# Attention by head pairs on fp16 high and low halves, and experts in tiles of 640 rows

## The chip, the cores and the metric

One core of a Trainium2 chip runs the whole program. The metric is the device time in microseconds. Five engines work from queues of their own: TensorE (PE in the profile, its weight loads PEld), VectorE (DVE), ScalarE (ACT), GpSimd (POOL) and SyncE (SP, which here only starts transfers). Transfers run on 16 DMA engines that all queues share. Matrix products read SBUF and write PSUM, eight banks of 2 KB in each of 128 partitions; VectorE or ScalarE must bring the results out of it.

## The reference

Inputs q, k, v are fp32 of shape (8 batches, 8 heads, 576, 64). For each batch and head two attentions are added:

```
q_d, k_d, v_d = means over groups of 4 rows      # 144 rows
out_up    = repeat(softmax(q_d k_d^T / 8) v_d, 4)
out_local = softmax(q k^T / 8 where |i - j| < 4) v
x = (out_up + out_local) as (4608 tokens, 512)
e_idx  = argmax(x @ w_gate)                       # 8 experts
gate_w = softmax(x @ w_gate)[e_idx]; eom = sigmoid(x @ w_output_gate)
out[token] = gate_w * eom[e_idx] * (relu(x @ w1[e]) @ w2[e])   # w1 512x1024, w2 1024x512
```

Each token goes to the one expert that its largest logit names, so the gate's logits must be exact enough to keep the order of near ties. With the fixed inputs the reference sends 553, 637, 487, 619, 575, 566, 572 and 599 tokens to the experts.

## The kernel before

The program is written for a planner that tracks the buffers: it gives every engine its own order of instructions, starting from program order but bringing an instruction forward when its inputs and a free buffer are there in the planner's own account of time. On the chip each engine then takes its list in order. A pool's `bufs` says how many copies of a tile may be alive.

**Attention** (lines 213 to 314) runs over 8 batches and in each over 8 heads. `load_batch` (lines 184 to 211) brings one batch of q, k and v over the SP queue, one batch ahead; GpSimd casts q and k to fp16 (L198 to L201); v stays fp32 in six overlapping blocks of 128 rows. For each head TensorE transposes q and k (L226, L228), makes the local scores in six blocks of 102 by 96 (L239) and the scores of the means (L252, L254). ScalarE takes exponentials (L244, L257, L258), VectorE multiplies by a mask (L246). The products with v are fp32 (L249, L275 to L279); the means of v are fp32 products against a pooling matrix (L261), transposed again (L266, L267). The 144 coarse rows are split into fp16 high and low halves and spread to 576 rows by 14 matmuls with a 0/1 matrix (L296 to L303). VectorE normalizes and adds (L306 to L310). After 8 heads the batch goes to DRAM (L311).

**Gate** (`gate_tile`, lines 119 to 182): 36 tiles of 128 tokens read x back, transpose it in fp32, multiply by both gates in fp32 (L129), find the expert, count ranks with a triangular matrix (L163, L164), and scatter the scaled fp16 row to the expert's slots in `hx_xs` (L179), 1024 slots for each expert. A running count `r_run` ties every tile to the one before.

**Experts** (lines 319 to 361): all 1024 slots of each expert, in four blocks of 256 rows. Weights arrive as fp32 in a single staging tile (`wst`, bufs=1) and are cast by ScalarE (L325) and VectorE (L329). `pye` has one buffer, copied by VectorE (L359). Results go to `hx_ys`.

**Gather** (lines 362 to 367): 36 times, an indirect read of 128 rows of `hx_ys` and a plain write to `out`, through four buffers.

Of the kernel before, what the change touches and what calls it, by code (L numbers as in the profile page):

```python
# [8 lines left out]
F32 = mybir.dt.float32  # L10
F16 = mybir.dt.float16
BF16 = mybir.dt.bfloat16
I32 = mybir.dt.int32
U32 = mybir.dt.uint32
# [4 lines left out]

def _ap(t, ap_list, extra_off=0):  # L20
    return bass.AP(tensor=t.tensor, offset=t.offset + extra_off, ap=ap_list)


@with_exitstack
def kernel(
# [16 lines left out]
    CAP = 1024  # L42
    NB = 6
    BR = 96
    KJ = BR + 6
    SD = S // 4
    scale = 1.0 / (D ** 0.5)
    NSLOT = CAP * E
    NT = N // 128

    x_dram = nc.dram_tensor("hx_x", (N, Dm), F32, kind="Internal")
    xs_dram = nc.dram_tensor("hx_xs", (NSLOT, Dm), F16, kind="Internal")
    ys_dram = nc.dram_tensor("hx_ys", (NSLOT, Dm), F32, kind="Internal")

    x5 = x_dram.ap().rearrange("(b t r) (h d) -> b r t h d", b=B, t=NB, r=BR, h=H)
# [10 lines left out]
    maskL = cst.tile([128, NB, BR], F32)
    nc.gpsimd.memset(maskL, 1.0)
    nc.gpsimd.affine_select(out=maskL, in_=maskL, compare_op=ALU.is_ge, fill=0.0,
                            base=0, pattern=[[0, NB], [-1, BR]], channel_multiplier=1)
    nc.gpsimd.affine_select(out=maskL, in_=maskL, compare_op=ALU.is_ge, fill=0.0,  # L70
                            base=6, pattern=[[0, NB], [1, BR]], channel_multiplier=-1)
    nc.gpsimd.affine_select(out=maskL, in_=maskL, compare_op=ALU.is_ge, fill=0.0,
                            base=-3, pattern=[[96, NB], [0, BR]], channel_multiplier=1)
    nc.gpsimd.affine_select(out=maskL, in_=maskL, compare_op=ALU.is_ge, fill=0.0,
                            base=S + 2, pattern=[[-96, NB], [0, BR]], channel_multiplier=-1)

    rall = cst.tile([128, NB, BR], F16)
    nc.gpsimd.memset(rall, 0.0)
    nc.gpsimd.affine_select(out=rall.rearrange("p t (a r) -> p t a r", r=4),
                            in_=rall.rearrange("p t (a r) -> p t a r", r=4),  # L80
                            compare_op=ALU.not_equal, fill=1.0, base=0,
                            pattern=[[-24, NB], [-1, 24], [0, 4]], channel_multiplier=1)
    rall2 = cst.tile([128, BR], F16)
    nc.gpsimd.memset(rall2, 0.0)
    nc.gpsimd.affine_select(out=rall2.rearrange("p (a r) -> p a r", r=4),
                            in_=rall2.rearrange("p (a r) -> p a r", r=4),
                            compare_op=ALU.not_equal, fill=1.0, base=8,
                            pattern=[[-1, 24], [0, 4]], channel_multiplier=1)
    rb = cst.tile([128, 24], F32)
    nc.gpsimd.memset(rb, 0.25)  # L90
    nc.gpsimd.affine_select(out=rb, in_=rb, compare_op=ALU.is_ge, fill=0.0,
                            base=-3, pattern=[[-4, 24]], channel_multiplier=1)
    nc.gpsimd.affine_select(out=rb, in_=rb, compare_op=ALU.is_ge, fill=0.0,
                            base=6, pattern=[[4, 24]], channel_multiplier=-1)
    lstr = cst.tile([128, 128], BF16)
    make_upper_triangular(nc, lstr, val=1.0, diag=False)
    ones128 = cst.tile([128, 128], BF16)
    nc.gpsimd.memset(ones128, 1.0)
    iota8i = cst.tile([128, 8], I32)
    nc.gpsimd.iota(iota8i, pattern=[[1, 8]], base=0, channel_multiplier=0)  # L100
    iota8f = cst.tile([128, 8], F32)
    nc.vector.tensor_copy(iota8f, iota8i)
    wgc = cst.tile([128, 4, 2 * E], F32)
    nc.sync.dma_start(wgc[:, :, 0:E], moe_w_gate.rearrange("(c p) e -> p c e", p=128))
    nc.sync.dma_start(wgc[:, :, E:2 * E], moe_w_output_gate.rearrange("(c p) e -> p c e", p=128))
    pos_all = cst.tile([128, NT], I32)
    zf16 = cst.tile([128, Dm], F16)
    nc.vector.memset(zf16, 0.0)
    nc.sync.dma_start(xs_dram.ap()[0:NSLOT, :].rearrange("(a p) d -> p a d", p=128),
                      _ap(zf16, [zf16.ap[0], [0, NSLOT // 128], [1, Dm]]))  # L110
    r_run = cst.tile([128, E], F32)
    nc.vector.memset(r_run, 0.0)
# [6 lines left out]
    def gate_tile(m):  # L119
        x128 = sbA.tile([128, Dm], F32, tag="x128")  # L120
        nc.sync.dma_start(x128, x_rt[m])
        pxT = psA.tile([128, 4, 128], F32, tag="pgate")
        for c in range(4):
            nc.tensor.transpose(pxT[:, c, :], x128[:, 128 * c:128 * c + 128], id32)
        xTs = sbA.tile([128, 4, 128], F32, tag="xTs")
        nc.vector.tensor_copy(xTs, pxT)  # L126
        pg = psA.tile([128, 2 * E], F32, tag="pgate")
        for c in range(4):
            nc.tensor.matmul(pg, lhsT=xTs[:, c, :], rhs=wgc[:, c, :],  # L129
                             start=(c == 0), stop=(c == 3))  # L130
        nlm = sbA.tile([128, 1], F32, tag="nlm")
        nc.vector.reduce_max(nlm, pg[:, 0:E], axis=AX.X, negate=True)
        pe8 = sbA.tile([128, E], F32, tag="pe8")
        sume = sbA.tile([128, 1], F32, tag="sume")
        nc.scalar.activation(pe8, pg[:, 0:E], AF.Exp, bias=nlm, scale=1.0, accum_out=sume)
        eomx = sbA.tile([128, E], F32, tag="eomx")
        nc.scalar.activation(eomx, pg[:, E:2 * E], AF.Exp, scale=-1.0)
        gw = sbA.tile([128, 1], F32, tag="gw")
        nc.vector.tensor_scalar_add(sume, sume, 1e-9)
        nc.vector.reciprocal(gw, sume)  # L140
        nc.vector.tensor_scalar_add(eomx, eomx, 1.0)
        eom8 = sbA.tile([128, E], F32, tag="eom8")
        nc.vector.reciprocal(eom8, eomx)
        mx8 = sbA.tile([128, 8], F32, tag="mx8")
        mi8 = sbA.tile([128, 8], U32, tag="mi8")
        nc.vector.max_with_indices(mx8, mi8, pg[:, 0:E])
        ef = sbA.tile([128, 1], F32, tag="ef")
        nc.vector.tensor_copy(ef, mi8[:, 0:1])
        onehot = sbA.tile([128, E], F32, tag="onehot")
        nc.vector.tensor_scalar(onehot, iota8f, scalar1=ef, scalar2=None, op0=ALU.is_equal)  # L150
        onehotb = sbA.tile([128, E], BF16, tag="onehotb")
        nc.vector.tensor_copy(onehotb, onehot)
# [64 lines left out]
    for b in range(B):  # L217
        q16, k16, vblk = pend
        if b + 1 < B:
            pend = load_batch(b + 1)  # L220
# [91 lines left out]
        for m in range(NT):  # L312
            if (128 * m + 127) // S == b:
                gate_tile(m)
# [83 lines left out]
```

## Time and profile before

| what | value |
|---|---|
| time, median of 3 runs | 1258.67 us (1256.92 to 1260.21) |
| profiled execution, span from first to last instruction | 1255.6 us |
| PE, PEld busy | 991.5 us (79%), 768.4 us (61%) |
| DVE, ACT, POOL busy | 523.1 us (42%), 246.2 us (20%), 117.6 us (9%) |
| instructions on PE | 6520 |
| moved by DMA | 141.63 MB, mean 113 GB/s |

The profiled execution has no time of its own besides its span, which is 3.1 us below the median of the timed runs; what lies around the span is thus about 3 us. Busy time is the union of an engine's instructions. Since matmuls overlap in the pipeline, a group's mean duration is longer than the distance between two starts; distances are read from the timeline.

### The profile page before, as it was taken

The page shows a single profiled execution, that of the slowest core. Times are in us where ns is not written, and L with a number is a line of the kernel's source. Part 1 is how long each engine was busy: PE and PEld are TensorE (multiplying, and loading weights), DVE is VectorE, ACT ScalarE, POOL GpSimd, SP SyncE. Part 2 cuts the span into 40 slices and gives each one's busy share as a digit, 9 for nine tenths or more (in the row PEclk, how much of TensorE's full clock was granted, in tenths as well). Part 3 has the DMA queues.
Part 4 walks back from the last instruction along what each step waited for, and adds up shares of the span by engine and source line. Part 5 has one row for each costly group of instructions (what it writes and reads, how often), then busy time and mean ns, then how long its engine had stood idle before and what let it go on. Part 6 is the DMA issues. An engine that isn't in the chain of part 4 may idle for free. (4 is left out here: it accounts for less than half of the span.)

```text
span 1255.6 us, 16704 instructions
## 1 busy us (share of the span) xinstructions
PE 991.5 (79%) x6520; PEld 768.4 (61%) x6520; DVE 523.1 (42%) x2211; ACT 246.2 (20%) x437; POOL 117.6 (9%) x128
## 2 busy tenths in 40 slices
PE   0799998899999987998899999864599999999000
PEld 0577776777787776777678777743366666666000
DVE  0354445545545555555655554634132323332000
ACT  0212211211321212221121121100133333322000
POOL 2310011010010002001100000001000000000243
PEclk9999999999999999999999999999999999999655
DMA  9940534616424332051040101011246666631677
GB/s 315 187 90 1 137 84 85 149 34 164 96 90 91 77 115 93 10 131 65 10 103 14 30 22 51 19 44 56 72 150 209 205 217 212 218 131 68 204 238 227
DMA packets 180991, 141.63 MB, mean 113 GB/s; under 512 B 126768, under 2 KB 143152, under 8 KB 180912
## 3 DMA queue, kind: packets, MB, share of 16 engines
q1 hardware_dynamic: 176304, 126.40, 35.4%
q0 software_dynamic: 4608, 14.16, 4.0%
q8 instruction: 51, 0.84, 0.3%
q14 instruction: 28, 0.23, 0.1%
HBM read 91.78 MB, written 48.76 MB: 112 GB/s over the span
## 5 line engine op out<-in xcount | busy, mean ns | idle before, releaser
L249 PE MATMUL ploc<-vblk,atl 102*96 102x65 f32 x768 | 146.8, 371 | 3.8 <-DVE atl L246 2.7
L357 PE MATMUL pye<-w2sb,hs 128*128 128x512 f16 x512 | 126.3, 379 | 20.9 <-DVE yee L359 19.9
L249 PEld LDWEIGHTS ploc<-vblk,atl 102*96 102x96 f32 x768 | 130.5, 275 | 14.2 <-DVE atl L246 5.8
L359 DVE COPY yee<-pye 128x512 f32<-128x512 f32 x64 | 44.2, 690 | 181.4 <-PE pye L357 181.4
L349 PE MATMUL phT<-xgT,w1sb 128*128 128x256 f16 x1024 | 118.9, 275 | 0.8 <-DVE xgT L342 0.8
L349 PEld LDWEIGHTS <-w1sb 128*128 128x128 f16 x1024 | 101.1, 99 | 20.2 <-issue 1.0
L226 PE MATMUL pqkt<-id,q 128*64 128x128 f16 (+1 forms) x320 | 81.1, 303 | 32.5 <-POOL q L198 32.5
L261 PE MATMUL pvdt<-rb,vblk 128*64 128x24 f32 x768 | 98.7, 283 | 8.5 <-ACT edt L258 8.0
L353 ACT ACTIVATE hs<-phT 128x1024 f16<-128x1024 f32 x64 | 65.5, 1023 | 193.4 <-PE phT L349 193.4
L235 DVE TENSOR_REDUCE qkd<-qkT 64x288 f16<-64x1152 f16 x64 | 84.7, 1324 | 38.2 <-ACT qkT L233 33.3
L261 PEld LDWEIGHTS pvdt<-rb,vblk 128*64 128x64 f32 x768 | 88.5, 222 | 17.5 <-ACT edt L258 12.6
L179 POOL DMA_INDIRECT hx_xs<-x16r,posi x36 | 35.1, 976 | 600.5 <-DVE pos_all L178 364.3
L357 PEld LDWEIGHTS <-hs 128*128 128x128 f16 x512 | 47.4, 97 | 69.5 <-issue 24.8
L233 ACT COPY qkT<-pqkt 64x1152 f16<-64x1152 f16 x64 | 70.8, 1106 | 82.6 <-PE pqkt L228 58.0
L296 PE MATMUL pup<-odh,rall 128*96 128x64 f16 x384 | 74.3, 265 | 15.5 <-DVE odh L290 10.4
L228 PE MATMUL pqkt<-id,k 128*64 128x128 f16 (+1 forms) x320 | 80.0, 299 | 5.4 <-POOL k L200 5.4
L129 PE MATMUL pg<-wgc,xTs 128*128 128x16 f32 x288 | 67.9, 376 | 16.2 <-DVE xTs L126 13.9
L129 PEld LDWEIGHTS pg<-wgc,xTs 128*128 128x128 f32 x288 | 64.2, 328 | 26.1 <-DVE xTs L126 20.9
L226 PEld LDWEIGHTS <-q 128*64 128x64 f16 (+1 forms) x320 | 47.9, 153 | 51.9 <-POOL q L198 32.5
L257 ACT ACTIVATE edt<-psd 128x144 f32<-128x144 f32 x64 | 18.5, 290 | 301.9 <-PE psd L254 301.9
L244 ACT ACTIVATE etl<-pst 102x576 f32<-102x576 f32 x64 | 41.5, 649 | 155.8 <-PE pst L239 148.9
L298 PE MATMUL pup<-odl,rall 128*96 128x64 f16 x384 | 69.5, 270 | 0.0
(116 smaller groups left out, 1456.6 us busy)
## 6 DMA issues: line engine op xcount, KB each, us to landing
w1st<-in_moe_w_dram SPq DMA_DIRECT2D x8, 2048.0 KB
w2st<-in_moe_w_dram SPq DMA_DIRECT2D x8, 2048.0 KB
hx_ys<-yee SPq DMA_DIRECT2D x8, 2048.0 KB, 13.8
hx_x<-out_sb SPq DMA_DIRECT2D x8, 1152.0 KB, 6.4
x<-hx_x SPq DMA_DIRECT2D x36, 256.0 KB, 2.7
out_dram<-g SPq DMA_DIRECT2D x36, 256.0 KB, 3.5
hx_xs<-zf SPq DMA_DIRECT2D x1, 8192.0 KB
q_rows<-in_q_dram SPq DMA_DIRECT2D x32, 256.0 KB, 4.8
```

The lines of the kernel that those rows point to most:

```text
L129: nc.tensor.matmul(pg, lhsT=xTs[:, c, :], rhs=wgc[:, c, :], start=(c == 0), stop=(c == 3))
L226: nc.tensor.transpose(pqkt[0:64, 0, 128 * m:128 * m + cnt], q16[0:cnt, h, m, :], id16[0:cnt, 0:cnt])
L228: nc.tensor.transpose(pqkt[0:64, 1, 128 * m:128 * m + cnt], k16[0:cnt, h, m, :], id16[0:cnt, 0:cnt])
L233: nc.scalar.copy(qkT[:, :, 3:579], pqkt[0:64, :, 0:576])
L235: nc.vector.tensor_reduce(qkd, qkT[:, :, 3:579].rearrange("p s (a r) -> p s a r", r=4), axis=AX.X, op=ALU.add)
L249: nc.tensor.matmul(ploc[:, t, :], lhsT=atl[0:KJ, t, :], rhs=vblk[0:KJ, h, t, :], start=True, stop=True)
L261: nc.tensor.matmul(pvdt[:, 24 * t:24 * t + 24], lhsT=vblk[:, h, t, 0:D], rhs=rb, start=True, stop=True)
L296: nc.tensor.matmul(pup[:, t, :], lhsT=rall[:, t, :], rhs=odh[0:128, 0, :], start=True, stop=False)
L298: nc.tensor.matmul(pup[:, t, :], lhsT=rall[:, t, :], rhs=odl[0:128, 0, :], start=False, stop=(t < 5))
L349: nc.tensor.matmul(phT[:, f4, :], lhsT=w1sb[:, c, 128 * f:128 * f + 128], rhs=xgT[:, :, c, :], start=(c == 0), stop=(c == 3))
L353: nc.scalar.activation(hs[:, 4 * half:4 * half + 4, :], phT, AF.Relu)
L357: nc.tensor.matmul(pye[:, rh, :], lhsT=hs[:, f, 128 * rh:128 * rh + 128], rhs=w2sb[:, f, :], start=(f == 0), stop=(f == E - 1))
```

## The change

Nearly the whole kernel is rewritten. The core of it, with `...` for what is left out:

```diff
+W = 112
+NB = 5
+Q0 = [0, 120, 232, 344, 456]
+QN = [120, 112, 112, 112, 120]
+CAPJ = 5
...
-    nc.sync.dma_start(xs_dram.ap()[0:NSLOT, :].rearrange("(a p) d -> p a d", p=128), ...
+    for r in range(E):                                  # 640 rows of 1032 bytes each
+        nc.scalar.dma_start(xs_dram.ap()[r * REG:r * REG + 128 * CAPJ, :]..., zt ...)
+    def load_weights(e):                                # wpool bufs=3
+        nc.gpsimd.dma_start(w1sb, moe_w1[e]...)         # fp32 in DRAM, fp16 in SBUF
+        nc.gpsimd.dma_start(w2sb, moe_w2[e]...)
+    def attn_pair(b, hp, vh, vdh, vdl, xo, vl):
+        pool_ps = psA.tile([128, 2, SD], F32, tag="M")
+        for i, src in enumerate((q, k)):
+            f = sbA.tile([96, 6, 2, D], F32, tag=f"qk{i}", bufs=3)
+            for h in range(2):
+                nc.sync.dma_start(f[:, :, h, :], src[b, h0 + h]...)
+            nc.gpsimd.tensor_copy(s16, f...)            # 96x768 to fp16
+            tp = psA.tile([128, S], F16, tag="T", bufs=2)
+            for m in range(6):
+                nc.tensor.transpose(tp[:, 96 * m:96 * m + 96], s16[:, m, :], id16[0:96, 0:96])
+            for m in range(6):
+                nc.tensor.matmul(pool_ps[:, i, 24 * m:24 * m + 24], lhsT=s16[:, m, :], rhs=pb[0:96, 0:24], ...)
+            nc.vector.tensor_copy(sT, tp)
+        nc.scalar.copy(qkd, pool_ps)
+        for h in range(2):       # pa: 1 mask matmul of 456 columns, 4 of about 114
+        for h in range(2):       # pbt: 1 mask matmul of 408, then 120, 144 and 144
...
+            nc.scalar.activation(E32[:, 0:NA], sc[h][:, 0:NA], AF.Exp, scale=scale)   # NA = 456
+            nc.scalar.activation(eh[:, 0:NA], sc[h][:, 0:NA], AF.Exp, scale=scale)
+            nc.scalar.activation(E32[:, NA:], pbt[:, 0:NBt], AF.Exp, scale=scale)     # NBt = 408
+            nc.scalar.activation(eh[:, NA:], pbt[:, 0:NBt], AF.Exp, scale=scale)
+            if h == 0:
+                nc.gpsimd.tensor_tensor(el, E32, eh, op=ALU.subtract)                 # 128x864
+            else:
+                nc.vector.tensor_tensor(el, E32, eh, op=ALU.subtract)
+            po = psA.tile([128, NB + 2, 65], F32, tag="O", bufs=2)
+            # 5 blocks x 3 and 2 x 2 x 3 matmuls, 64 or 65 columns: eh*vh, eh*vl, el*vh
+            nc.vector.reciprocal(rs, po[:, :, 64])
+            nc.vector.tensor_tensor(xo[:, :, D * hh:D * hh + D], po[:, :, 0:D], _bc(rs, D), op=ALU.mult)
+    def gate(b, xo):
+        for t in range(NB):      # spread of the coarse rows, SBUF to SBUF, 6 transfers
+            nc.sync.dma_start(up[0:4 * n, t, :], _ap(src, [src.ap[0], [0, 4], [1, Dm]]))
+        nc.vector.tensor_tensor(x, x, up, op=ALU.add)                                 # 120x2560
+        nc.scalar.copy(xh[0:BR, :, 0:Dm], x)
+        nc.gpsimd.tensor_tensor(xl[0:BR], x, xh[0:BR, :, 0:Dm], op=ALU.subtract)
+        # for t in 5: 8 transposes, 1 copy by VectorE, 8 matmuls of 32 or 16 columns
+        # then once for all 5: about 20 small operations of VectorE, 3 of ScalarE,
+        # 6 rank matmuls
+        for t in range(NB):
+            nc.gpsimd.indirect_dma_start(out=xs_dram.ap(), ... pos[:, t:t + 1] ..., in_=xh[0:P, t, :]...)
+    for b in range(B):
+        # per pair: 2 loads of v; GpSimd writes vh, VectorE vl
+        # 12 matmuls of 512 columns against pv: the means of v for all 8 heads
+        for hp in range(NP):
+            attn_pair(b, hp, vh, vd1h, vdl, xo, vl)
+        gate(b, xo)
+        if b < 3:
+            load_weights(b)
+    def experts(xgi, nj, w1sb, w2sb, group):            # nj = 5: 640 rows
+        # 20 transposes, 3 copies; 8 x 2 x 4 matmuls of 320 columns, buffers U bufs=4,
+        # relu by ScalarE for one half and VectorE for the other; 5 x 8 matmuls of 512
+        nc.scalar.activation(y[:, j, :], py, AF.Copy, scale=coef[:, j, 0:1])          # Y bufs=2
+        nc.gpsimd.indirect_dma_start(out=out_rows, ..., in_=y[:, j, :], ..., bounds_check=N - 1, oob_is_err=False)
+    for e in range(E):
+        if e not in wts:
+            load_weights(e)
+        nc.sync.dma_start(xg, xs_dram.ap()[base:base + 128 * CAPJ, :]...)
+        experts(xg, CAPJ, *wts[e], True)
+    v_most = nc.values_load(most[0:1, 0:1], ...)
+    with tc.If(v_most > 0):      # for an expert with more than 640 tokens: loops over more tiles
...
-        for m in range(NT):      # gather and write of out, and all of gate_tile, are gone
```

Every fp32 operand of a matmul is now the sum of two fp16 tiles. v is scaled by 1024 and split in `vh` (GpSimd) and `vl` (VectorE); the exponentials are made twice by ScalarE, in fp32 and in fp16, and their difference is the low half. The mask is added to the scores inside PSUM, by a matmul of the identity with a constant. Two heads lie side by side in the 128 partitions. The transposed q and k are not pooled by VectorE; TensorE pools the fp16 rows. x stays in SBUF. The row that is scattered to an expert is unscaled fp16 with the coefficient and the token's number behind it, and the expert's output is scaled, and scattered by that number, straight to `out`.

## Rows read from the trace of the kernel before

**Rows 1.** Busy time in five stretches; columns: stretch, its length, engines, granted clock, DMA share, GB/s.
```profile
0.00:32.50 32.50, 0.01 (x1) 0.01 (x1) 2.95 (x15) 1.28 (x1) 9.98 (x26) 1.00 1.07 312
32.50:840.00 807.50, 725.59 (x4658) 588.36 (x4658) 425.39 (x1974) 156.35 (x351) 68.46 (x62) 1.00 0.31 75
840.00:892.00 52.00, 16.01 (x70) 13.19 (x70) 18.19 (x121) 2.12 (x15) 4.83 (x5) 1.00 0.27 83
892.00:1165.00 273.00, 249.84 (x1792) 166.81 (x1792) 76.56 (x102) 86.44 (x70) 0.00 (x0) 1.00 0.48 166
1165.00:1255.60 90.60, 0.00 (x0) 0.00 (x0) 0.06 (x1) 0.00 (x0) 34.32 (x36) 0.52 0.75 232
```

**Rows 2.** Timeline of PE; columns: start us, us, engine, line, operation, shapes, count.
```profile
420.01 2.18 PE L249 MATMUL ploc<-vblk,atl 102*96 102x65 f32 x12
...
423.14 0.27 PE L296 MATMUL pup<-odh,rall 128*96 128x64 f16 x1
423.22 0.27 PE L298 MATMUL pup<-odl,rall 128*96 128x64 f16 x1
...
868.22 0.17 PE L163 MATMUL pcnt<-onehotb,lstr 128*128 128x8 bf16 x1 [2.08 <-DVE eomsel L155]
868.25 0.17 PE L164 MATMUL pcnt<-onehotb,ones 128*128 128x8 bf16 x1
...
902.17 0.39 PE L339 MATMUL pxg<-id,xg 128*128 128x128 f16 x4
...
913.15 3.66 PE L349 MATMUL phT<-xgT,w1sb 128*128 128x256 f16 x32
...
919.74 1.89 PE L357 MATMUL pye<-w2sb,hs 128*128 128x512 f16 x8 [0.56 <-DVE yee L359]
```

**Rows 3.** Groups of DVE by line and shape; columns: busy us, mean ns, idle before, releasers.
```profile
L359 DVE COPY yee<-pye 128x512 f32<-128x512 f32 x64 | 44.2, 690 | 181.4 <-PE pye L357 181.4
L246 DVE TENSOR_TENSOR atl<-etl,maskL 102x576 f32<-102x576 f32 x64 | 48.2, 753 | 17.2 <-ACT etl L244 17.0
L342 DVE COPY xgT<-pxg 128x1024 f16<-128x1024 f16 x32 | 21.8, 680 | 10.1 <-PE pxg L339 10.1
L132 DVE TENSOR_REDUCE nlm<-pg 128x1 f32<-128x8 f32 x36 | 6.0, 166 | 58.5 <-PE pg L129 58.4
```

**Rows 4.** Groups of ACT by line and shape.
```profile
L244 ACT ACTIVATE etl<-pst 102x576 f32<-102x576 f32 x64 | 41.5, 649 | 155.8 <-PE pst L239 148.9 <-DVE out_sb L309 6.2 <-DVE sume L139 0.6
L325 ACT CAST w1sb<-w1st 128x4096 f16<-128x4096 f32 x8 | 28.8, 3596 | 0.0
```

**Rows 5.** Groups of POOL by line and shape, and shortest, median, longest of L198.
```profile
L179 POOL DMA_INDIRECT hx_xs<-x16r,posi x36 | 35.1, 976 | 600.5 <-DVE pos_all L178 364.3 <-DVE posi L177 191.8 <-DVE rdu L284 12.1
L198 POOL CAST q<-q_rows 128x2048 f16<-128x2048 f32 x8 | 15.4, 1925 | 190.7 <-issue 132.9 <-DMA q_rows<-in_q_dram 34.4 <-PE pqkt L226 23.4
L199 POOL CAST q<-q_rows 64x512 f16<-64x512 f32 x8 | 5.6, 694 | 0.0
L79 POOL TENSOR_SCALAR_AFFINE_SELECT rall<-rall 128x576 f16<-128x576 f16 x1 | 1.8, 1773 | 0.0
...
L198 POOL CAST q<-q_rows x8: 1889/1890/2162, 30.5 to 594.7; 128x2048 f16<-128x2048 f32 x8
```

**Rows 6.** Transfers: issues of SP, pieces of the chain, and all packets.
```profile
41.61 4.48 SPq L192 DMA_DIRECT2D q_rows<-in_q_dram  x4
...
883.87 2.42 DMA hx_xs<-x16r,posi
...
886.73 5.81 DMA xg<-hx_xs
...
962.96 9.69 DMA w2st<-in_moe_w_dram
...
DMA packets 180991, 141.63 MB, mean 113 GB/s; under 512 B 126768, under 2 KB 143152, under 8 KB 180912
```

**Rows 7.** Timeline: the last gather.
```profile
1247.44 0.95 POOL L364 DMA_INDIRECT g<-hx_ys,pos_all  x1 [1.29 <-DMA out_dram<-g]
```

More of the change, by code (lines that the diff above doesn't have):

```diff
@@ L41 @@
     F = moe_w1.shape[2]
[L42 to L45, printed above, removed]
     SD = S // 4
+    NP = H // 2
+    NG = F // 128
+    XW = Dm + 4
+    REG = N
     scale = 1.0 / (D ** 0.5)
[L48 to L55, printed above, removed]
@@ L64 @@
     make_identity(nc, id16)
[L66 to L92, printed above, removed]
@@ L103 @@
[L103 to L110, printed above, removed]
@@ new lines @@
+    nc.vector.scalar_tensor_tensor(wg[:, :, 2 * E:4 * E], in0=wgf, scalar=GS, in1=wg[:, :, 0:2 * E],
+                                   op0=ALU.mult, op1=ALU.subtract)
+    vh_s, xh_s, w9_s = [], [], []
+    for i in range(2):
+        t_vh = cst.tile([128, H, NB, 66], F16, tag=f"vh{i}")
+        nc.vector.memset(t_vh[:, :, :, 64:66], 0.25)
+        vh_s.append(t_vh)
+        t_xh = cst.tile([128, NB, XW], F16, tag=f"xh{i}")
+        nc.vector.memset(t_xh, 0.0)
+        xh_s.append(t_xh)
+        t_w9 = cst.tile([128, NB, E + 1], F32, tag=f"w9{i}")
+        nc.vector.memset(t_w9, 0.0)
+        nc.gpsimd.affine_select(out=t_w9[:, 1:NB - 1, E:E + 1], in_=t_w9[:, 1:NB - 1, E:E + 1],
+                                compare_op=ALU.is_ge, fill=float(E + 1), base=W - 1,
+                                pattern=[[0, NB - 2], [0, 1]], channel_multiplier=-1)
+        w9_s.append(t_w9)
@@ L114 @@
+    low = nc.allow_low_precision("split in high and low halves, or exact")
+    low.__enter__()
+    wts = {}
+    def load_weights(e):
+        w1sb = wpool.tile([128, 4, F], F16, tag="w1")
+        nc.gpsimd.dma_start(w1sb, moe_w1[e].rearrange("(c p) f -> p c f", p=128))
+        w2sb = wpool.tile([128, NG, Dm], F16, tag="w2")
+        nc.gpsimd.dma_start(w2sb, moe_w2[e].rearrange("(g p) j -> p g j", p=128))
+        wts[e] = (w1sb, w2sb)
     sbA_cm = tc.tile_pool(name="sbA", bufs=2)
@@ new lines @@
+    more = cst.tile([128, E], I32)
+    nc.vector.tensor_scalar(more, cntf, scalar1=127.0 - 128.0 * CAPJ, scalar2=0.0, op0=ALU.add, op1=ALU.max)
+    nc.vector.tensor_scalar(more, more, scalar1=7, scalar2=None, op0=ALU.arith_shift_right)
+    most = cst.tile([128, 1], I32)
+    nc.vector.tensor_reduce(most, more, axis=AX.X, op=ALU.max)
+    sbF = ctx.enter_context(tc.tile_pool(name="sbF", bufs=2))
+    psF = ctx.enter_context(tc.tile_pool(name="psF", bufs=1, space=bass.MemoryType.PSUM))
+    out_rows = out
@@ L371 @@
+    low.__exit__(None, None, None)
 _INS = ['q', 'k', 'v', 'moe_w_gate', 'moe_w_output_gate', 'moe_w1', 'moe_w2']
```

535 lines of the change are left out of this document (277 added, 258 removed).

## The prediction

> **What bounds the kernel now.** I read the busy times by stretch first [rows 1]. The reader is to see five stages: 32.5 us of loading, 807.5 us of attention with gates, 52.0 us in which the last gates run alone, 273.0 us of experts and 90.6 us of gathering. In attention PE is busy 725.59 of 807.50 us, 90%, and DVE, the next, 53%: PE bounds it, 101 us a batch. In the experts PE is busy 249.84 of 273.0 us. In the other three stages PE does next to nothing.
>
> The timeline of PE tells what an instruction costs there, as the distance between starts [rows 2]. Twelve fp32 products of 65 columns take 2.18 us; taking 0.37 us off for the last one's pipeline, they start 0.165 us apart. fp16 products with 96 stationary columns start 80 ns apart. With 128 stationary columns it is 57 ns for 128 moving columns ((0.39 - 0.22)/3), 109 ns for 256 ((3.66 - 0.27)/31), 216 ns for 512 ((1.89 - 0.38)/7), and 30 ns for the two of 8 columns. So a short fp16 product with a full stationary tile costs 30 to 57 ns, a third of the fp32 one or less.
>
> **The change stage by stage**, in a batch of four pairs (eight heads) for attention.
>
> *PE.* A head has 6 transposes at 57 ns, 6 pooling products at 40, 9 score and mask products of 192 columns on average (between 57 and 109 ns, 85 taken) and 27 products with v of 64 or 65 columns. For these I take 45 ns, between the 30 and the 57 of [rows 2]; the far end is the 80 ns of the 96-column stationary tile. That is 0.34 + 0.24 + 0.77 + 1.22 = 2.57 us, 20.5 us a batch. The means of v are 12 products at 216 ns, 2.6 us; the gate 40 transposes, 40 products and 6 ranks, 4.1 us. Sum 27.3 us a batch, or 41 us with 80 ns for all short ones ((12 x 0.080 + 0.85 + 2.16) x 8 + 2.6 + 6.9).
>
> A rule speaks on those 27 products: the Trainium skill, TensorE: Matmul & The Clock Gate, "Weight-path perf modes", says that a stationary tile of exactly 128 columns that is not fp32 is loaded by a faster path. The trace agrees: 96 columns cost 80 ns and 128 columns 30 to 57. Without that path, by the same page's plain rule of one column per 1.2 GHz cycle, 48 instructions at 107 ns would make about 50 us a batch, an estimate.
>
> *DVE*, from [rows 3]. A pair: two copies of 128x576 fp16 out of PSUM (0.68 us for 1024, so 0.45 each), the low half of v (640 elements at 0.753/576 us, 0.84), one difference of 864 (1.13), and for each head a reciprocal (0.19) and the normalized write (448 of the 0.69 us for 512, 0.60): 0.90 + 0.84 + 1.13 + 1.58 = 4.5 us, 18 a batch. Once a batch: two copies of 512 (1.4), the sum of 2560 (3.35), five copies of 1024 (3.4) and some 20 small ones at 0.17 (3.4). Sum 29.5 us.
>
> *ACT*, from [rows 4]: 0.84 ns an element and 0.17 us fixed, by the two rows. A head has two exponentials of 456 and two of 408, 2.12 us; a pair also one copy of 288, 0.41: 18.6 us a batch. With two copies of 512 (1.2), one cast of 2560 (2.3) and three small ones 22.7 us.
>
> *POOL*, from [rows 5]. Casts lie on 0.80 ns an element plus 0.28 us: 768 elements 0.90 us, twice a pair, and vh 0.80. What no row shows is a GpSimd operation on two tensors: `el` of every other head (864 elements) and `xl` (2560). From below 0.92 ns an element, the cast's total rate; from above 3.08, the slowest one-input operation there (L79, 1773 ns for 576). I take 2.0, the middle: 1.75 and 5.1 us. With five scatters at 0.976: 17.4 + 5.1 + 4.9 = 27.4 us a batch, from 20.8 to 33.8 by the two ends.
>
> By a page alone there is a price: the Trainium skill, GPSIMD Engine Reference, "Performance versus the Vector engine", measures 4497 ns for a two-tensor add of 2048; by that the sum would be 28.5 us, an estimate.
>
> So four engines come to 27.3, 29.5, 22.7 and 27.4 us a batch, where before PE had nearly the whole and the rest had slack. How much of the largest becomes time? Before, one engine filled 90% of its stage. Now each pair passes load, GpSimd, PE, VectorE, PE, ScalarE (four exponentials), GpSimd or VectorE, PE, VectorE, about 11.5 us in a row (from the prices above), and two pairs are in flight; M, the bank of the pooled scores, has one buffer, and the gate's logits and ranks use it too. Three waits are new and have work behind them: the six spread transfers on SP wait for the batch's last normalized write, with the next loads of q, k and v behind them (three pairs' worth are ahead, so PE need not notice); `el` on GpSimd waits for ScalarE, with the next pair's casts behind it, and PE waits for those; `xl` and the scatters hold the same queue for 10 us a batch. I take a fill of 0.72, midway between 0.90 and 0.55: 41 us a batch, 328 us for eight. The ends are 262 and 429 us.
>
> The transfers fit under that: q, k, v, the spread, the scatters, the zero rows and three experts' weights are some 64 MB; in 345 us that is 185 GB/s, where the first stretch moved 312 [rows 1].
>
> *Start.* The 8 MB of zero rows no longer stand before q on the SP queue. v of one batch and the first pair's q and k, 1.9 MB, at the 1 MB in 4.48 us of [rows 6] take 8 us; with issue, landing and a cast, 16 us instead of 32.5. GpSimd's constants, 9.98 us in that stretch [rows 1], I price at nothing, since the first cast's data lands after them; if theirs grow beyond 15 us, each further one counts.
>
> *Last gate*, which nothing hides, as nothing hid the 52.0 us before: spread 8, sum 3.4, cast 2.3, `xl` 5.1, the five transposes and copies 5, small operations and ranks 4, scatters 4.9 and landing 2.4, the first rows of the expert 4 (640 of the 1024 rows that took 5.81) [rows 6]: 39 us. Ends: 30 and 44.
>
> *Experts.* 20 transposes at 57 ns, 64 products of 320 columns at 136 (109 x 320/256), 40 at 216: 1.1 + 8.7 + 8.6 = 18.5 us, where before 32, 128 and 64 made 29.6 of 34.1. Of the 4.5 us lost I keep 1, since results now have two buffers and weights three; the other engines have 7 to 12 us an expert. 156 us, 2 for the first copy: 158. Ends: 150 and 184.
>
> Here the weights of experts 3 to 7 must stay hidden. Two weight tiles of 2 MB need about 19.4 us at 9.69 each [rows 6]; the load for expert 3 may start when expert 0 frees its tiles, three experts ahead, so it arrives in time if the conversion on the way costs no more than the plain load. No row shows a converting transfer; below nothing is excluded, since it never stands on the path, and above, at half the rate, see the rivals.
>
> *Tail.* The 90.6 us of gathering go. Late instead: last write from PSUM 0.7, a scatter 0.98 and 2.42 to land, and an end like that after the last gather, 8.2 us from 1247.44 to 1255.6 [rows 7]; the reading of the register and the branch I put inside it, up to 10 us if they are not. 13 us; ends 9 and 23.
>
> Sum: 16 + 328 + 39 + 158 + 13 = 554 us of span, against 1255.6 in the profiled execution. The median of the timed runs is 3.1 us above that span, so 557 us.
>
> **Rivals.** *GpSimd becomes the bound.* At the upper price it has 33.8 us a batch, and VectorE's operations on two SBUF tensors (11.2 us a batch: vl, el, the sum) may hold it up. For: `el`, `xl` and casts share one queue. Against: of the eight casts at L198 the median equals the shortest, 1.89 us, and only the longest, 2.16, is stretched [rows 5]. Price: 45 us, at 0.9 fill 50 a batch, 400 us; total 629. The Trainium skill, GPSIMD Engine Reference, "Specifications", states that the SBUF interfaces are shared with VectorE and contend with its operations on two SBUF inputs; that one stretched cast is all the trace shows of it. Chance 0.20.
>
> *Converting loads at half rate.* 39 us an expert; five from the release at 10 us land at 204, and the last expert's work follows: 223 instead of 158 us; total 622. Against: the DMA engines were only 0.48 busy in the experts [rows 1]. Chance 0.14.
>
> *PE at its upper price*, by 80 ns short products or by the lower clock. For: with gaps in attention the grant may fall, as it did to 0.52, near the lower level of 1.2 GHz, where PE idled; against, it was 1.00 through 840 to 892 us with PE busy 16 of 52 [rows 1]. 41 to 55 us, at 0.85 to 0.9 fill 48 to 61 a batch: 610 to 720. Chance 0.10.
>
> *The branch is taken*, so that the fixed tiles don't do what they say: the largest expert has 637 of 640 rows by the reference; if four tokens near a tie move there, eight loads of weights (155 us) and a tile follow, about 750. Chance 0.03.
>
> *Slower than before.* The converting loads go element by element. Before, 180991 packets took 40% of 16 engines' time (the shares of [rows 1], weighted), 44 ns each. An expert has 1.05 million weights; such packets would take 2.9 ms on 16 engines. The change turns into a loss once each of the five loads on the path lasts 160 us, 58,000 packets or 72 bytes of fp32 each. For: more than two thirds of today's packets are under 512 bytes [rows 6]; against: the weights' rows are contiguous 2 and 4 KB. Chance 0.03.
>
> **Numbers.** The forecast has 0.50, with an own range of 470 to 610. The range, 470 to 690, leaves out the lowest tenth of the forecast, the worst part of PE's rival, the branch and the loss, together under 0.2. A difference of 0.3%, 4 us, is about what a measurement of this kernel can tell from none. All cases but the last are faster by more: 0.96 faster, 0.01 same, 0.03 slower.
>
> **What would show it.** First transposes at 16 us; batches 41 us apart, with no engine over 80% busy; if POOL is near full there, the first rival; 27 products of a head in 1.2 us, or 2.2 for the third. Experts 19.5 us apart; PE waiting on w1 from the fourth on shows the second rival. From the last PE instruction to the end 13 us. A batch over 50 us, an expert over 25, or a start after 25 would make the prediction wrong.

## The result, and the profile after

The changed kernel takes 779.42 us (median; 778.19 to 786.13), the kernel before 1258.98: a ratio of 0.6203, 95% interval 0.6178 to 0.6228. Forecast were 557 us, range 470 to 690: the sign was right, the time lies outside, 222 us above the forecast. The profiled execution spans 778.80 us.

Its busy time by stretch, cut where the prediction cut, with the columns of [rows 1]: start, first batch, the seven other batches, last gate, experts, tail.

```profile
0.00:16.26 16.26, 1.26 (x3) 0.36 (x4) 7.74 (x18) 0.00 (x0) 15.24 (x42) 1.00 1.02 191
16.26:89.38 73.12, 43.25 (x399) 25.17 (x400) 22.60 (x35) 18.42 (x39) 32.49 (x26) 0.62 1.08 210
89.38:561.02 471.64, 308.42 (x3370) 201.73 (x3368) 205.66 (x409) 139.46 (x294) 229.08 (x146) 0.56 0.35 76
561.02:604.32 43.30, 6.58 (x88) 5.70 (x89) 9.27 (x29) 3.06 (x4) 10.05 (x6) 0.50 0.27 69
604.32:768.74 164.42, 155.24 (x992) 93.81 (x992) 44.61 (x88) 54.80 (x103) 46.77 (x49) 0.96 0.66 145
768.74:778.80 10.06, 0.00 (x0) 0.00 (x0) 0.00 (x0) 0.69 (x1) 1.21 (x2) 0.60 0.14 50
```

The reader is to set each length against the prediction's term: start 16.26 against 16, first batch 73.1 against 41, seven batches 471.6 against 287 (67.4 each), last gate 43.3 against 39, experts 164.4 against 158, tail 10.1 against 13. The two attention terms hold 217 of the 225 us by which the span was missed. In the seven batches PE, the busiest engine, is busy 65% of the time, where it had 90% [rows 1]; and its granted clock, 1.00 before, is 0.56.

Between two batches, the timeline of the kernel after (start us, us, engine, line, operation, and in brackets the idle time before it with its releaser):

```profile
430.01 0.62 DVE L244 TENSOR_TENSOR xo<-po,rs 128x448 f32<-128x448 f32 x1
...
430.66 4.93 SPq L253 DMA_DIRECT2D up<-xo  x5
...
439.99 2.83 DVE L258 TENSOR_TENSOR xo<-xo,up 120x2560 f32<-120x2560 f32 x1 [4.76 <-DMA up<-xo]
440.81 3.67 POOL L345 TENSOR_SCALAR t_vh<-vf 128x640 f16<-128x640 f32 x1 [15.76 <-DMA f<-in_k_dram]
442.85 2.33 ACT L259 CAST t_xh<-xo 120x2560 f16<-120x2560 f32 x1 [8.41 <-DVE xo L258]
...
445.23 1.04 PE L265 MATMUL tp<-id,t_xh 128*128 128x128 f16 x8 [11.40 <-ACT t_xh L259]
445.26 5.03 POOL L260 TENSOR_TENSOR t_xl<-xo,t_xh 120x2560 f16<-120x2560 f32 x1 [0.77 <-ACT t_xh L259]
...
450.34 1.03 PE L267 MATMUL tp<-id,t_xl 128*128 128x128 f16 x8 [4.07 <-POOL t_xl L260]
...
460.09 0.17 DVE L328 TENSOR_TENSOR pos<-m,rsel 120x5 int32<-120x5 f32 x1
...
460.35 0.82 POOL L177 CAST s<-f 96x768 f16<-96x768 f32 x1 [10.07 <-PE pool_ps L182]
```

The gate is a chain, and PE stands in it: last normalized write, six spread transfers, sum, cast, `xl`, transposes. PE idles 11.40 us for the cast and 4.07 for `xl`, because its list has the gate's transposes ahead of the next batch. In the 29.7 us from 430.63 to 460.35 PE is busy 12.54. It is so in each batch. From 89 to 561 us PE's two waits are (us in total, times, longest):

```profile
PE tp L265 <- ACT t_xh L259: 84.4, 7, 12.9
PE tp L267 <- POOL t_xl L260: 28.5, 7, 4.1
```

The groups over the whole kernel, with the last gate in them (busy us, mean ns, idle before, releaser):

```profile
L265 PE MATMUL tp<-id,t_xh 128*128 128x128 f16 x160 | 22.2, 303 | 100.1 <-ACT t_xh L259 100.1
L231 PE MATMUL po<-t_vh,el 128*128 128x65 f16 x320 | 57.5, 243 | 34.9 <-POOL el L222 34.2 <-DVE el L224 0.2
L267 PE MATMUL tp<-id,t_xl 128*128 128x128 f16 x160 | 23.2, 310 | 32.6 <-POOL t_xl L260 32.6
L345 POOL TENSOR_SCALAR t_vh<-vf 128x640 f16<-128x640 f32 x32 | 68.5, 2142 | 98.1 <-DMA f<-in_k_dram 64.3 <-DMA vf<-in_v_dram 18.8 <-PE po L231 13.4
L224 DVE TENSOR_TENSOR el<-E,eh 128x864 f16<-128x864 f32 x32 | 44.7, 1398 | 13.7 <-ACT eh L220 13.1
L222 POOL TENSOR_TENSOR el<-E,eh 128x864 f16<-128x864 f32 x32 | 58.4, 1826 | 20.1 <-ACT eh L220 19.4
L399 PE MATMUL pu<-xgT,w1sb 128*128 128x320 f16 x512 | 73.7, 306 | 1.8 <-DVE xgT L391 1.5 <-DMA out_dram<-y,xg 0.2
```

The clock, by stretches of the same kernel in which PE was busy without a gap: short products of attention twice, then an expert's products of 320 columns.

```profile
70.00:80.00 10.00, 10.00 (x113) 6.69 (x110) 4.09 (x8) 5.25 (x11) 3.03 (x2) 0.50 1.14 206
540.00:550.00 10.00, 9.99 (x121) 6.91 (x118) 4.51 (x9) 4.91 (x12) 2.27 (x2) 0.50 0.00 0
612.00:620.00 8.00, 8.00 (x54) 5.07 (x52) 2.95 (x6) 2.87 (x6) 0.85 (x1) 1.00 0.11 10
```

So the low level, 1.2 GHz, was not granted for idling here. The ends of products are modelled, so I count columns too: those that start between 540 and 550 us are 10336, which at 1.2 GHz fill 8.6 of the 10 us (an estimate from the timeline). The products with v then start 54 ns apart:

```profile
403.05 0.24 PE L231 MATMUL po<-vl,eh 128*128 128x64 f16 x1
403.10 0.24 PE L231 MATMUL po<-t_vh,el 128*128 128x65 f16 x1
403.15 0.25 PE L231 MATMUL po<-t_vh,eh 128*128 128x65 f16 x1
403.21 0.24 PE L231 MATMUL po<-vl,eh 128*128 128x64 f16 x1
```

### The profile page after: what moved, and what is told of

Read it like the earlier page. It is cut to its first block, busy times and chain, and to the rows that moved or that the text cites. A ratio compares the mean times of both kernels' runs of the same rounds, so it can differ in the third digit from the quotient of the medians.

```text
span 778.8 us, 12008 instructions
## 1 busy us (share of the span) xinstructions
PE 514.8 (66%) x4849; PEld 326.8 (42%) x4849; DVE 289.9 (37%) x577; ACT 216.4 (28%) x441; POOL 334.8 (43%) x269
## 5 line engine op out<-in xcount | busy, mean ns | idle before, releaser
L345 POOL TENSOR_SCALAR t_vh<-vf 128x640 f16<-128x640 f32 x32 | 68.5, 2142 | 98.1 <-DMA f<-in_k_dram 64.3
L177 POOL CAST s<-f 96x768 f16<-96x768 f32 x64 | 66.1, 1045 | 98.7 <-PE pool_ps L182 59.2
L265 PE MATMUL tp<-id,t_xh 128*128 128x128 f16 x160 | 22.2, 303 | 100.1 <-ACT t_xh L259 100.1
L399 PE MATMUL pu<-xgT,w1sb 128*128 128x320 f16 x512 | 73.7, 306 | 1.8 <-DVE xgT L391 1.5
L409 PE MATMUL py<-w2sb,hs 128*128 128x512 f16 x320 | 70.4, 379 | 0.0
L222 POOL TENSOR_TENSOR el<-E,eh 128x864 f16<-128x864 f32 x32 | 58.4, 1826 | 20.1 <-ACT eh L220 19.4
L231 PE MATMUL po<-t_vh,eh 128*128 128x65 f16 x320 | 61.0, 244 | 7.6 <-ACT eh L218 6.7
L238 PE MATMUL po<-vd1h,el 128*128 128x65 f16 (+1 forms) x256 | 62.0, 242 | 0.0
L238 PE MATMUL po<-vdl,eh 128*128 128x64 f16 (+1 forms) x256 | 61.5, 240 | 0.0
L231 PE MATMUL po<-vl,eh 128*128 128x64 f16 x320 | 60.7, 242 | 0.0
L238 PE MATMUL po<-vd1h,eh 128*128 128x65 f16 (+1 forms) x256 | 60.1, 235 | 0.0
## 6 DMA issues: line engine op xcount, KB each, us to landing
w1sb<-in_moe_w_dram POOLq DMA_DIRECT2D x8, 1024.0 KB, 10.6
```

Of the source, the lines that this page charges most:

```text
L177: nc.gpsimd.tensor_copy(s16, f.rearrange("p m h d -> p m (h d)"))
L222: nc.gpsimd.tensor_tensor(el, E32, eh, op=ALU.subtract)
L231: mm = nc.tensor.matmul(po[:, t, 0:n], lhsT=a[:, c], rhs=bm[:, hh, t, 0:n], start=(a is eh and bm is vh), stop=(a is el), skip_group_check ...
L238: mm = nc.tensor.matmul(po[:, g, 0:n], lhsT=a[0:kn, c], rhs=bm[0:kn, kc, hh, 0:n], start=(kc == 0 and a is eh and bm is vdh), stop=(kc == ...
L265: nc.tensor.transpose(tp[:, c, :], xh[:, t, 128 * c:128 * c + 128], id16)
L345: nc.gpsimd.tensor_scalar(vh[:, hs, :, 0:D], vf, scalar1=VS, scalar2=None, op0=ALU.mult)
```

## The experiments

Theory A: the seven gates that the prediction took as hidden are on the path. Rival B: PE's low clock makes the pairs themselves long. Both can be true; the runs are to say how much of the miss each has. Each run is compared with the changed kernel, 779.42 us, or with the run that it is built on.

**No gate.**

```diff
-        gate(b, xo)
+        if b == B - 1:
+            gate(b, xo)
```

> Leaves out the gates and the scatters of the first seven batches (their rows of the output stay unwritten by the experts). Theory A, the order: PE's list puts the gate of a batch between its last pair and the next batch, so seven gates stand on the path; the batches then come 40 us apart instead of 67.4 and the time falls by about 190 us, to 590. Theory B, the clock: PE works at half its clock (granted 0.50 even where it is busy without a gap) because its products are short, and needs some 43 us a batch by itself; the time falls as far, but the granted clock in attention stays near 0.5. If instead the gate's gaps make the clock fall, it goes to 0.9 or more here and the batches come under 36 us apart, time under 560.

Measured: 581.87 us, ratio 0.4625 (0.4616 to 0.4635), 198 us less. From the end of the first batch to the last normalized write:

```profile
89.38:371.72 282.34, 248.01 (x2741) 151.32 (x2739) 134.20 (x232) 118.13 (x265) 160.64 (x102) 0.65 0.44 77
```

A batch of pairs takes 40.3 us, PE 88% busy, and with the gate gone the clock is still 0.65; so the gate's gaps alone don't make it low. Both theories had forecast this time, so the time doesn't choose between them. The stretch says what the seven gates cost: it is 189 us shorter, of which 60 are PE's own work (308.42 us busy with gates, 248.01 without) and 129 are idle time of PE; the two waits above are 113 us. And it says that B is there too: the pairs alone keep PE busy 35.4 us a batch (248.01/7).

**Gate later:** batch b's gate behind the second pair of batch b+1.

```diff
+            if hp == 1 and b > 0:
+                gate(b - 1, xo_prev)
-        gate(b, xo)
+        xo_prev = xo
+    gate(B - 1, xo_prev)
```

> The gate of batch b is written behind the second pair of batch b+1, nothing else. Theory A: PE no longer stands 11.4 us before the gate's transposes and 4.1 before those of the low half, batches 50 us apart, time about 660. Rival: the one bank M, which the gate's logits and ranks share with the pooled scores, holds the next pairs back all the same; PE's waits move to the pooling products, time above 740. If gaps make the clock fall, the granted clock rises to 0.8 or more and the time goes to 620.

Measured: 705.9 us (0.5574 to 0.5653), between the two expectations; the sums of two batches come about 56 us apart. PE's waits for the cast fall from 100.1 us to the last batch's, and others grow:

```profile
L231 PE MATMUL po<-t_vh,el 128*128 128x65 f16 x320 | 54.9, 237 | 55.2 <-POOL el L222 42.6 <-DVE el L224 12.6
...
L265 PE MATMUL tp<-id,t_xh 128*128 128x128 f16 x160 | 22.5, 301 | 15.7 <-ACT t_xh L259 15.7
```

73 us of the 198 come back. Of the 124 that are left, some 38 are PE's own work for the gates (busy 285.64 us from the first batch's sum to the last's, beside 248.01 without gates); the rest is waiting, on `el` and elsewhere.

**Wide masks**, with and without the gates: each mask product, 456 or 408 columns, is made four times over.

```diff
+            for _ in range(4):
-            nc.tensor.matmul(pa[:, 0:NA], lhsT=id16, rhs=mk[:, 0:NA], start=True, stop=False,
+                nc.tensor.matmul(pa[:, 0:NA], lhsT=id16, rhs=mk[:, 0:NA], start=True, stop=False,
...                                                     # pbt likewise
```

> Each mask product (456 and 408 columns) is made four times instead of once, to the same result: 2592 columns more a head, 8.6 us a batch at 2.4 GHz and 17 at 1.2. Theory B, the short products keep the clock low: wide ones raise it, to 0.8 or more in attention, and the products with v start 30 to 45 ns apart instead of 54; the time falls a little in spite of the work, to 700 to 770. Rival, the gaps of the gate keep it low: the clock stays at 0.5 and the time rises by 80 to 130 us, to 860 to 910.

> Without the first seven gates (as in the run without gates) and with every mask product made four times. Theory B in its strong form: there PE, busy 88% at a mean clock of 0.62, is bound by its low clock; the wide products raise it above 0.8, and 20 us of work at full clock plus 8.6 are less than the 38 us a batch, time 520 to 560 instead of 582. Rival: what the clock gives back the columns take; time 582 to 640 although the clock rises.

Measured: 823.39 us with gates (0.6499 to 0.6574), 610.61 without (0.4812 to 0.4895): 44 and 29 us more. With gates neither expectation came: the clock in the seven batches rose from 0.56 to 0.72, not to 0.8, and the time rose less than the rival had it. Without gates the rival's time came, and the clock rises:

```profile
100.00:400.00 300.00, 275.42 (x3020) 156.63 (x3018) 129.33 (x227) 124.16 (x263) 156.82 (x100) 0.86 0.36 72
```

At a clock of 0.95 in this run (200 to 204 us) the products with v start 30 ns apart, against 54:

```profile
202.49 0.19 PE L233 MATMUL po<-t_vh,el 128*128 128x65 f16 x1
202.52 0.19 PE L233 MATMUL po<-t_vh,eh 128*128 128x65 f16 x1
202.55 0.20 PE L233 MATMUL po<-vl,eh 128*128 128x64 f16 x1
```

So wider products raise the clock, and here their columns cost more than it gives back. The Trainium skill, TensorE: Matmul & The Clock Gate, "Wait — 56ns, not 53.3ns?", gives the distance as columns by the clock, plus 2.5 ns at the upper level: 54 and 30 ns for 65 columns, as estimates; the trace agrees.

**The start.** Zero rows issued by SP behind batch 0's pairs, or the first three experts' weights only when a batch's last normalized write is done.

```diff
-        nc.scalar.dma_start(
...
+        if b == 0:
...
+                nc.sync.dma_start(
```

> The zero rows go from the SP queue, written behind the first batch's means of v, instead of from ScalarE's queue at the start, where their issue holds ScalarE until 35.5 us. Theory: the first exponentials come 15 us earlier, time 760 to 768. Rival: the DMA engines are full until 80 us with weights and zero rows, so the second pair's q and k come as late as before, time within 5 us of 779.

```diff
+        if after is not None:
+            nc.vector.tensor_copy(w1sb[0:1, 0, 0:1], after)
...                                                     # w2sb likewise
-            load_weights(b)
+            load_weights(b, xo[0:1, 0, Dm - 1:Dm])
```

> The first three experts' weights are loaded only once the last head of batch 0, 1 or 2 is written, by a copy of one element of that head into the weight tile ahead of the load. Theory: their 12 MB before 80 us keep q and k of the first pairs away; the first batch's sum comes at 75 to 85 us instead of 98.9, time 755 to 765. Rival: ScalarE, held by the zero rows until 35.5 us, sets the start; time within 5 us of 779.

Measured: 788.97 us (0.6249 to 0.6283) with the zero rows on SP, against both expectations. ScalarE is free, and its first exponential comes at 19.86 us instead of 38.00:

```profile
19.86 0.55 ACT L213 ACTIVATE E<-pa 128x456 f32<-128x456 f32 x1 [0.56 <-PE pa L195]
```

Yet the batch's sum comes at 106.8 us instead of 98.9. So ScalarE's held queue is not what made the first batch long. With late weights it is 772.3 us (0.6094 to 0.6158), between the expectations, and the first sum comes at 82.1: the weights do compete with the first batch's loads. Of the 17 us won there 7 reach the end. The seven next batches take 474 us, as before (472); 8 us are lost behind the last sum, among the experts, where PE now waits 6.29 and 5.96 us for the rows of two of them.

**Banks.** Two buffers for M at the cost of one of S (three to two), with the gate later and with the gate in its place.

```diff
-        pool_ps = psA.tile([128, 2, SD], F32, tag="M")
+        pool_ps = psA.tile([128, 2, SD], F32, tag="M", bufs=2)
-            pa = psA.tile([128, 512], F32, tag="S", bufs=3)
+            pa = psA.tile([128, 512], F32, tag="S", bufs=2)
...                                                     # pbt, lg, rk and cnt likewise
```

> As the run with the gate behind the second pair, and bank M has two buffers (the score banks S two instead of three). Theory C: there the next pairs' pooling products waited for the gate's logits to leave M (GpSimd stood 12 us a batch behind them, ScalarE 13 us), so batches come under 50 us apart instead of 56, time 640 to 665. Rival: the waits come from the order of the lists alone, or S with two buffers costs as much; time within 10 us of 706 or above.

> Only the banks: M two buffers, S two, the gate where it was. If the place of the gate in PE's list is the first cause and M the second, PE still stands 15 us a batch before the gate's transposes and the time stays within 770 to 785. If M alone kept the next batch's pairs from running beside the gate, the time falls below 740.

Measured: 724.63 (0.5681 to 0.5772) and 803.34 us (0.6364 to 0.6397), 19 and 24 us worse; the first is the rival's result, the second above both expectations. ScalarE's waits for `pbt`, which lies in S, rise from 36.5 to 103.1 us in the second. The lost buffer of S thus hides what M's second one may give, and M stays open. So the next run leaves S alone and puts the gate's logits and ranks into O's two banks:

```diff
-        lg = psA.tile([128, NB, 4 * E], F32, tag="M")
+        lg = psA.tile([128, NB, 4 * E], F32, tag="O", bufs=2)
...
-        rk = psA.tile([128, NB, E], F32, tag="M")
+        rk = psA.tile([128, NB, E], F32, tag="O", bufs=2)
```

> The gate behind the second pair, S with three buffers as in the change, and the gate's logits and ranks in the two banks O of the outputs instead of M. It repeats the test of theory C without taking a buffer from the scores. If M was what held the next pairs, batches come under 50 us apart, time 640 to 680. If not, within 10 us of 706, or above, where the logits hold up an output bank.

Measured: 684.66 us (0.5404 to 0.546), 21 less than the later gate alone: the shared bank was a part. It was not all of it: the sums come 52.5 us apart, not under 50, and the time lies between the expectations.

**Stages and GpSimd's list.** The gate cut in three (spread to `xl`; products; the rest), a part behind each of the next batch's first three pairs; `vh` and `xl` on VectorE; then stages, banks O and late weights together, without and with `vh` on VectorE.

```diff
+        yield
         lg = psA.tile([128, NB, 4 * E], F32, tag="M")
...
+                if hp in (0, 1, 2):
+                    next(g, None)
```

> The gate is cut in three: spread, sum and halves behind the first pair of the next batch, transposes and logits behind the second, ranks and scatters behind the third. Theory A carried on: of the 56 us a batch that were left, 38 are the pairs; part of the other 18 is ScalarE standing 13 us before the logits' copy and the pairs' exponentials behind it, so batches come under 50 us apart, time 640 to 670. Rival: the 18 are the gate's own products at the low clock, some 8 us, and GpSimd's operations; time 690 to 706.

```diff
-            nc.gpsimd.tensor_scalar(vh[:, hs, :, 0:D], vf, scalar1=VS, scalar2=None, op0=ALU.mult)
+            nc.vector.tensor_scalar(vh[:, hs, :, 0:D], vf, scalar1=VS, scalar2=None, op0=ALU.mult)
-        nc.gpsimd.tensor_tensor(xl[0:BR], x, xh[0:BR, :, 0:Dm], op=ALU.subtract)
+        nc.vector.tensor_tensor(xl[0:BR], x, xh[0:BR, :, 0:Dm], op=ALU.subtract)
```

> The gate behind the second pair, and vh and xl made by VectorE instead of GpSimd. Theory D: vh took 1.81 us or more instead of the 0.80 of the prediction, 8 us a batch, and xl 5.0; in front of el in GpSimd's list they make PE wait 8 us a batch for el and xl. Without them 46 to 50 us a batch, time 640 to 665. Rival: VectorE, busy 28 to 33 of 50 us there, is late instead; time within 10 us of 706.

> Three edits together: the gate in three stages, its logits and ranks in the banks O, and the first weights after the first batch. Theory A: each alone gave 19 to 21 us over the moved gate or 7 over the change; if the lists still hold PE up, the sum is 660 to 670. Theory B: what is left is PE's products at the low clock (busy 42 of 53 us a batch), the edits take away the same waits, and the time stays at 675 to 685.

> The same with vh on VectorE. If GpSimd's list still makes PE wait for el, 5 to 15 us less than the run before; if PE's low clock bounds, no difference, within 5 us.

Measured, in this order:

- stages alone 686.64 us (0.5375 to 0.5449), 19 less than the later gate, between the expectations;
- `vh` and `xl` on VectorE 695.34 (0.5501 to 0.5539), 11 less than the later gate and far from theory D's 640 to 665;
- the three edits together 681.89 (0.5405 to 0.5427), as theory B had it: stages and banks O each give some 20 us, but not one on top of the other;
- the same with `vh` on VectorE 663.81 (0.5228 to 0.5288), 18 less, somewhat more than theory A's 5 to 15. So PE's low clock is not all that holds this kernel, against theory B of the run before.

**Less work on PE**, on the later gate with banks O, and on the pairs alone; last, `vh` on VectorE on the pairs alone.

```diff
-                for a, bm, n in ((eh, vh, 65), (eh, vl, 64), (el, vh, 65)):
+                for a, bm, n in ((eh, vh, 65), (el, vh, 65)):
...                                                     # vdh, vdl likewise
```

> The kernel with the gate behind the second pair and its logits in O (684.7 us), with the products with the low halves of v and of its means left out, 9 of 27 a head, which nothing waits for; so the output lacks the low half of v. At 54 ns a product that is 3.9 us of PE a batch, 31 in all. Theory B, PE at its low clock bounds these batches: time 650 to 660. Theory A, waits in the lists bound them: the time falls by less than 12 us, to 673 to 685.

> The kernel without the first seven gates and their scatters, and in it each head without the nine products of the low half of v (18 of 27 stay); its output lacks both. Removed on PE: 64 x 9 products at 54 ns, the distance of their starts at the granted clock of 0.50, 31 us in all. Theory A (without the gates PE is the bound: 248.01 of 282.34 us busy from the first batch's end to the last's, 88%): most of it comes back, 552 to 562 us from 581.87. Rival (even there the pairs wait for each other in the lists of PE, GpSimd and ScalarE): under 10 us, 572 to 582, with PE busy under 80% of its batches.

> The kernel without the first seven gates and their scatters, with the high half of v written by VectorE; its output lacks the seven gates. GpSimd loses 32 operations of 2.1 us, VectorE gains 32 of about 0.5. Theory A (PE is the bound of the pairs alone): within 5 us of 581.87 after the first batch, 575 to 587. Rival (GpSimd's list sets the pairs' pace, as it did with the gates in stages, where the same edit gave 18 us): 560 to 572.

Measured: 675.51 (0.5317 to 0.5381), 572.19 (0.4539 to 0.4562) and 578.73 us (0.4575 to 0.4615). 31 us less of PE gave 9 and 10 us back, and `vh` gave 3, hardly more than the spread of the runs. In the pairs alone the clock fell as the products went; first the kernel without gates, then the same without those products:

```profile
100.00:330.00 230.00, 203.13 (x2223) 124.14 (x2222) 108.15 (x187) 95.04 (x214) 139.50 (x87) 0.63 0.50 87
```

```profile
100.00:330.00 230.00, 200.35 (x1840) 111.36 (x1837) 108.59 (x197) 95.03 (x215) 135.47 (x92) 0.56 0.56 93
```

PE is as busy as before (88 and 87%), at 0.56 instead of 0.63: of the two expectations the time fits the rival, the busy share theory A. That the lower clock took the gain is the reading that fits these rows; no run held the clock fixed. With the gates, PE waited 33.8 us for VectorE's `el`, where it had waited 4.8 before the products went, and two rows of that run's timeline say why:

```profile
263.99 5.02 POOL L260 TENSOR_TENSOR t_xl<-xo,t_xh 120x2560 f16<-120x2560 f32 x1
```

```profile
264.15 5.77 DVE L224 TENSOR_TENSOR el<-E,eh 128x864 f16<-128x864 f32 x1
```

`el` takes 1.06 us where GpSimd is still; begun 0.16 us after `xl`, it ends 0.91 us after it. Six batches of this run show the same 5.77 us or 5.76. In these pairs of subtractions, on two SBUF tensors each, the engines take turns. Not every overlap is such a turn: in the kernel after, an `el` that begins while GpSimd scales `vh`, from one tensor, is not longer.

```profile
154.16 1.81 POOL L345 TENSOR_SCALAR t_vh<-vf 128x640 f16<-128x640 f32 x1
```

```profile
155.19 1.06 DVE L224 TENSOR_TENSOR el<-E,eh 128x864 f16<-128x864 f32 x1 [1.26 <-ACT eh L220]
```

**Without that turn:** `xl` on VectorE (the edit above), in the kernel with less PE work and in the one with stages, banks O, late weights and `vh` on VectorE.

> The kernel with the gate behind the second pair, logits and ranks in banks O, without the nine products of the low half of v (its output lacks them), and with xl written by VectorE. Without that last edit VectorE's el, 1.06 us alone, took 5.77 us beside GpSimd's xl (5.02 us) once a batch, and PE waited 33.8 us for it in all. Theory A (VectorE's operations on two SBUF tensors and GpSimd's operations take turns, and that turn ate what PE had gained): no el over 2.5 us, PE's wait for VectorE's el under 15 us, and 645 to 662 us where it was 675.51. Rival (the turns only fill time in which PE waits for something else): el is short, PE's wait moves to GpSimd's el or the casts, 668 to 680.

> The kernel with the gate in stages, logits and ranks in banks O, late weights, vh on VectorE, and now xl on VectorE too: 8 x 2.8 us more there, 8 x 5.0 less on GpSimd. Theory A (the two engines' turns cost time on the path once a batch): 640 to 656 from 663.81. Rival (VectorE, 197 of 300 us busy already, gets the 2.8 us a batch into PE's path): 658 to 675.

Measured: 656.53 us (0.5206 to 0.5233), 19 less, PE's wait for that `el` 4.7 us (the longest `el` is 3.08, over the 2.5 expected); and 654.88 us (0.5203 to 0.5222), 9 less, with intervals that only just miss each other. Both times are theory A's. What the edit does besides, it doesn't separate: on VectorE `xl` itself takes 2.8 us instead of 5.0, and GpSimd's list is shorter by it. The second is the fastest complete version, ahead of both kernels.

## Why the prediction was wrong

The step that failed is in the paragraph on four engines: the new waits "have work behind them", and for the spread "three pairs' worth are ahead, so PE need not notice", from which came "a fill of 0.72". It named what queues on SP and GpSimd and left out PE's own list, in which the gate's transposes stand between a batch's last pair and the next batch's first score products. The last gate alone was priced as exposed, at 39 us; all eight are. In the seven batches PE stands 113 us before the gate's transposes, and without the seven gates the kernel takes 581.87 us, 198 less.

Not all of the 198 is miss, since the forecast's 41 us a batch held the gate's work too. By its own method (the largest engine without the gate, PE at 23.2, over 0.72) the pairs alone would come to 32 us a batch, which leaves 9 for the gate; this is an estimate from its terms. Measured are 40.3 and 27. So of the 26 us by which a batch was too long, some 18 belong to the gate and 8 to the price of the pairs: about 127 and 57 us in seven batches. The start has another 32.

*The start.* 16 us to the first transposes was right (16.26), but the first batch took 73.1 us instead of 41. The prediction spread the transfers evenly over attention, at 185 GB/s. The zero rows and weights that no longer stood before q stood beside it: the DMA share in that stretch is 1.08 at 210 GB/s. Late weights won 17 of the 32 us at the first sum. ScalarE's timeline shows its queue issuing the zero rows until 35.43 us, and its first exponential behind that:

```profile
9.80 25.63 ACTq L145 DMA_DIRECT2D hx_xs<-zt  x8
...
38.00 0.54 ACT L217 ACTIVATE E<-pa 128x456 f32<-128x456 f32 x1
```

But the run that freed ScalarE's queue was slower, so this is no cause shown; what holds the other 15 us stays open.

*PE's price* was mis-sized, by the clock. The sum took [rows 2], all at 1.00; after, PE is busy 35.4 us in a batch of pairs without the gate (248.01/7) where 27.3 - 4.1 = 23.2 were priced (23.2 over the 0.65 granted is 36), and the gate adds 8.6 (60.4/7) where 4.1 were. That the pairs alone came out at 40.3 us, beside the 41 that were forecast for pairs and gate, is luck: PE cost half as much again, and filled 0.88 of the time and not 0.72. The 27 products of a head take 1.5 us at 54 ns, between the 1.2 and the 2.2 that were to tell forecast and third rival apart. The third rival had the lower clock, but for gaps, and [rows 1] seemed to speak against it; it came with full work of short products.

*GpSimd* was priced well for `el` and `xl` (1.83 and 5.03 us, predicted 1.75 and 5.1), badly for `vh`: 1.81 us at best and 2.14 in the mean for 0.80, 43 us in 32. The first rival was false as put, with GpSimd 49% busy in the seven batches (229.08 of 471.64); its condition, that VectorE's operations on two SBUF tensors hold it up, was true in part. I had dismissed it on [rows 5], where only casts ran beside VectorE. In the kernel after, VectorE's `el` is 10.8 us over 32 times 1.06 and `vh` 10.6 us over 32 times 1.81.

*Right:* the experts, the tail and the last gate within 7 us each. VectorE's and ScalarE's rows held for the new shapes: 0.62 us for `xo` (0.60), 2.33 for the cast (2.3). Converting loads were not slow, the second rival: 10.6 and 11.0 us from issue to landing beside 9.69 [rows 6], and PE's products with w1 waited 1.8 us in all. The branch was not taken, and the loss by small elements did not come.

What stays open: no run set the clock without adding or taking columns, so what the pairs would take at 1.00 with the same work isn't shown; nor is how far the 655 us of the fastest version could come down. The 582 without gates is no mark to reach, since the gates' own products are missing there.

## What to carry to other kernels

For every new dependent chain, read the program order of the engine that bounds the stage: what it must execute next in its own list, not only what is queued behind the waiting transfer, decides whether the chain is hidden. Put such a chain's consumers a pair or two later in that list, in parts, and look again at which banks and queues they share. Price work on GpSimd together with what VectorE does at that moment, and short products of TensorE at both clock levels.

## What the hardware did that was not expected

- TensorE was granted 0.50 through 10 us of 65-column and other short fp16 products, with PE busy 9.99 us of them, and 1.00 in the 320-column ones. Without the gates, three more wide products at each mask brought 0.86; taking nine short ones a head away brought 0.56 from 0.63, with PE 88 and 87% busy.
- A VectorE subtraction of two SBUF tensors (1.06 us) took 5.77 us beside a GpSimd subtraction of 5.02. The other way, GpSimd's `vh` (1.81 us) took 3.67 when VectorE's sum of 2.83 began 0.82 us ahead of it. The Trainium skill, GPSIMD Engine Reference, "Specifications", says that GpSimd shares its SBUF interfaces with VectorE and contends with its operations on two SBUF inputs; the trace agrees, and shows the later one waiting nearly all that is left of the other's operation. Beside GpSimd's `vh`, begun earlier, an `el` of VectorE took its usual 1.06 us.
- Eight DMA issues of zero rows held ScalarE's queue for 25.63 us, and with it the engine's first exponentials; for 17.15 us where the first weights came later. Freeing the queue won nothing: the first batch ended 8 us later.
